# Two orders of small work around the second block of a fused retention and ELU layer kernel: where the last weight sums are made, and which ScalarE work goes first at the change of layers

## The chip, the cores and the metric

The kernel runs on one core of one Trainium2 chip. The metric is the device time of one execution in microseconds; the time before is the median of six runs. In the profile the engines are PE (TensorE: matrix products; PEld its weight loads), DVE (VectorE), ACT (ScalarE), POOL (GpSimd) and SP, which here only issues DMAs. "L532" is line 532 of the kernel before. Every engine carries out its own list of instructions strictly in the order in which the program emits them, and waits where an operand, or the buffer that it writes, is not ready.

## The reference

For each of 4 batches and 8 heads (768 positions, 64 dimensions) a state is decayed and fed, and read by the query; the heads are then put side by side to 3072 tokens of 512, and two dense layers with an ELU between them follow:

```python
for t in range(S):
    state = gamma[None, :, None, None] * state + np.einsum('bhd,bhe->bhde', k[:, :, t], v[:, :, t])
    y[:, :, t] = scale * np.einsum('bhd,bhde->bhe', q[:, :, t], state)
x = np.ascontiguousarray(attn_out.transpose(0, 2, 1, 3)).reshape(B * S, H * D)
h = x @ w_in                                                     # 512 -> 2048
g = np.where(h > 0.0, h, alpha * (np.exp(np.minimum(h, 0.0)) - 1.0))
return (g @ w_out).astype(np.float32)                            # 2048 -> 512
```

All of it is float32.

## The kernel before

The 3072 tokens are cut into six blocks of 512 tokens. For each block the retention makes `xb` (the block's input, transposed), the first layer with its ELU makes the inner values `gq`, and the second layer makes 512 outputs per token. All instructions are emitted in an order written out by hand with Python generators: a `next(...)` emits the work up to the next `yield`, so the place of a `next` decides where that work stands in every engine's list. There is no scheduler.

Block 0 uses plain products (`plain_first`, `plain_second`). While `plain_second` runs, the output weights arrive in eight pieces (`n` = 0 to 7), are decoded on DVE, and are combined there into the sums that later blocks need. From block 1 on, each product of two matrices is done in seven products of half the size instead of eight, after the Strassen-Winograd scheme. This needs sums of weight quarters (made once) and sums of input quarters.

The second layer goes one level deeper: each of its seven products is itself done in seven small products. The weights of these small products are sums of sums. `combine_w_out(at, low, high)` (L524 on) makes them for two neighbouring pieces: eight DVE `tensor_tensor` instructions (helper line L532), a `yield` after each, and at the end of each four the stores to a scratch tensor are put in the list `to_send` (issued by SP from L528). For the last pair of pieces (`at` = 3) four instructions of 128x512 come first (called s1 to s4 here, tile `wi`), and then four of 128x384 (m1 to m4). In the kernel before, L509 emits the first two of them, s1 and s2, at the end of the last step of `plain_second`, ahead of the copies of the last two output banks that fall to DVE (L519). The other six are left in `held["last"]`.

Block 1's first layer is four "quadruples" (`first(n)`, n = 0 to 3, each two row blocks of the inner layer), each by the general seven-product generator `strassen` (L587). It emits product 1, product 2, 6, 7, 5, then stops at `yield "gap"`, and later product 3, product 4, a plain `yield "last"`, and the last ELU of the quadruple, that of the quarter C21. The helpers:

- `kept(ps)` (L575): ACT copies a PSUM bank to a tile `m`, so that the bank or the sum can be used on.
- `plus(ps, m)` (L580): DVE adds a bank and a kept tile into `h`. It frees the bank.
- `elu(g, h)`: two ACT instructions (L444, L445), and an instruction on DVE that finishes the ELU (L448), which is put into `later` and emitted one ELU later, or by `flush()`.
- `combine_w_in(n)` (L559): four DVE sums of input weights for quadruple n.
- `combine_small(j)` (L700): eight POOL instructions in all on the input weights, after the last `combine_w_in`; L637 makes two sums on DVE of each quadruple's results.

The banks in use are a (two buffers), b and d. Products 1, 6, 5, 3 add up in one buffer of bank a; products 7 and 4 add up in bank d. So product 5 can start only when ACT has copied the sum of products 1 and 6, and product 7 of the next quadruple only when `plus` (L580) has read bank d after product 4 of this one.

The loop over quadruples runs the last part of quadruple n - 1 (`tail`: products 3 and 4 with their ELUs) after products 1 and 2 of quadruple n, and hands out two steps of `sides[n]` per product:

```python
sides = [
    itertools.chain(combine_w_in(1), last), itertools.chain(combine_w_in(2), combine_w_in(3)), iter(()), iter(()),
]
```

So in quadruple 0 DVE's list has the four sums of `combine_w_in(1)` and then what is left of `last`, with the `plus` and ELU instructions of the quadruple between them. `send_small()` issues the stores at the end of the quadruple.

After quadruple 3, the second layer starts with `second_twice(1, ...)`. Its first large product j = 1 has the small products 1 and 2, then 6 and 7, then 5, and so on (`inner`, matmuls at L834, ACT copies `ms` at L842, DVE sums at L846). The order at the change of layers in the kernel before is: small products 1 and 2, the tail of quadruple 3 with products 3 and 4 and its last ELU, `flush()`, then small products 6 and 7, and then 5.

Of the kernel before, what the change touches and what calls it, by code (L numbers as in the profile page):

```python
# [17 lines left out]
def kernel(  # L18
# [47 lines left out]
    NF = DFF // P // 2  # L66
# [350 lines left out]
    def combine_x_parts():  # L417
        sub = lambda o, x, y: nc.vector.tensor_tensor(out=o, in0=x, in1=y, op=ALU.subtract)
        b11, b12, b21, b22 = (xb[:, 2 * r : 2 * r + 2, half[t]] for r in range(2) for t in range(2))
        sub(xt[0], b12, b11)  # L420
        yield
        sub(xt[1], b22, xt[0])
        yield
        sub(xt[2], b22, b12)
        yield
        sub(xt[3], b21, xt[1])
# [8 lines left out]
    def flush():  # L435
        while later:
            later.pop(0)()
# [46 lines left out]
    def plain_second():  # L484

        ops = [bank(x).rearrange("p a b -> p (a b)") for x in "aabd"]
        for n, f in enumerate(ORDER_F):
            wo = decoded[2 * NQ + n]
            for row in range(2):
                for d in range(4):  # L490
                    nc.tensor.matmul(  # L491
                        ops[d], lhsT=wo[:, row, (d if row else d ^ 2) * P :][:, 0:P], rhs=g_plain[row * NF + f],
                        start=(n == 0 and row == 0), stop=(n == NF - 1 and row == 1),
                    )
            so = t4.tile([P, 4, 256], FP32, name="so", tag="t4")
            tt = lambda o, x, y, op: nc.vector.tensor_tensor(out=o, in0=x, in1=y, op=op)
            a21, a11, a12, a22 = (wo[:, r, 256 * d : 256 * d + 256] for r in range(2) for d in range(2))
            tt(so[:, 0], a21, a22, ALU.add)
            tt(so[:, 1], so[:, 0], a11, ALU.subtract)
            tt(so[:, 2], a11, a21, ALU.subtract)  # L500
            tt(so[:, 3], a12, so[:, 1], ALU.subtract)
            nc.sync.dma_start(quarters(f)[:, 8:16], so.rearrange("p a (d c) -> p (a d) c", c=P))
            if n < 5:
                send_small()
            sources = wo.rearrange("p r (d c) -> p (r d) c", d=2)[:, 1:4], so
            if n % 2:
                last = combine_w_out(n // 2, low, sources)

                for _ in itertools.islice(last, 8 if n < NF - 1 else 2):  # L509
                    pass  # L510
            low = sources
            if n >= 5:
                send_small()
            held["last"] = last if n % 2 else None
            yield
        for d in range(4):
            ot = gq["T3"][:, 2 * d : 2 * d + 2, :]
            eng = (nc.scalar.copy, nc.vector.tensor_copy)[d % 2]
            eng(ot.rearrange("p a b -> p (a b)"), ops[d])  # L519
            nc.sync.dma_start(out[0, d // 2, :, :, d % 2, :].rearrange("t p c -> p t c"), ot)  # L520
# [5 lines left out]
    def send_small():  # L526
        while to_send:
            nc.sync.dma_start(*to_send.pop(0))  # L528

    def combine_w_out(at, low, high):  # L530

        tt = lambda o, x, y, op: nc.vector.tensor_tensor(out=o, in0=x, in1=y, op=op)  # L532
        if at < 3:

            ms = [mpool.tile([P, 2, TH], FP32, name="m", tag="m") for _ in range(4)]
            ms = [m.rearrange("p a (b c) -> p (a b) c", c=P)[:, 0:3] for m in ms]
            ss = gq["T3"].rearrange("p (k f) (b c) -> p k (f b) c", k=4, c=P)
        else:
            ms, ss = (stage.tile([P, 4, 4, P], FP32, name="wi", tag="stage") for _ in range(2))
            ms = [ms[:, k, 0:3] for k in range(4)]  # L540
        ss = [ss[:, k] for k in range(4)]
        for first, dst, k in [(0, ms, 0), (3, ss, 1)][:: 1 if at < 3 else -1]:
            a11, a21, a12, a22 = (x[k][:, :, P * d : P * d + P] for x in (low, high) for d in range(2))
            s1, s2, s3, s4 = dst
            tt(s1, a21, a22, ALU.add)
            yield
            tt(s2, s1, a11, ALU.subtract)
            yield
            tt(s3, a11, a21, ALU.subtract)
            yield  # L550
            tt(s4, a12, s2, ALU.subtract)
            to = scratch2[first : first + dst[0].shape[1]].rearrange("j p (k f c) -> k f p j c", k=4, f=4)
            for k in range(4):
                to_send.append((to[k, at], dst[k]))
            yield
# [14 lines left out]
    def bank(x):  # L570
        return ps_f.tile([P, 2, TH], FP32, name="p" + x, tag=x, bufs=2 if x == "a" else 1)
# [90 lines left out]
    for tb in range(1, NTB):  # L662
# [5 lines left out]
        for j in ORDER2:  # L668
            last = (4, 3) if j == 4 and tb == NTB - 1 else (3, 4)
# [377 lines left out]
    for n, _ in enumerate(plain_second()):  # L1047
        decode_all()
        prepare()
        if n == 1:  # L1050
            scores(1, 0)
            scores(1, 1)
        elif n == 2:
            states(1, 0)
            states(1, 1)
        elif 3 <= n <= 5:
            outputs_step(1, n - 3)
        elif n == 6:
            combine_x()
            for _ in combine_w_in(0):  # L1060
                pass
# [17 lines left out]
    tail = iter(())  # L1079
    last = held["last"]  # L1080
# [4 lines left out]
    for n in range(NQ):  # L1085
# [14 lines left out]
        tail = cur  # L1100
# [13 lines left out]
    sec = second_twice(1, combine_x_twice)  # L1114
    for _ in range(3):
        next(sec)
    for _ in tail:
        pass
    flush()
    next(sec)  # L1120
    for step, s in enumerate(sec):
        if step in (0, 2, 4, 5):
            retention_step(2, (1, 1, 2, 2, 3, 4)[step])
# [2 lines left out]
    tail = sec  # L1126


    for tb in range(2, NTB):
# [24 lines left out]
        tail, parts = iter(()), combine_x_parts()  # L1154
        for at, j in enumerate(TWICE):
# [14 lines left out]
            tail = cur  # L1170
# [3 lines left out]
        sec = second_twice(tb, combine_x_twice if more else lambda: None)  # L1174
# [47 lines left out]
        tail = sec  # L1222
# [51 lines left out]
```

## Time and profile before

| what | value |
|---|---|
| median of six runs (lowest, highest) | 645.17 us (643.9, 645.48) |
| the profiled execution's own time | 647.54 us |
| its span | 645.7 us |
| outside the span (the difference) | 1.84 us |
| PE busy | 635.1 us, 98% of the span |
| DVE busy | 498.1 us, 77% |
| ACT busy | 241.4 us, 37% |
| POOL busy | 40.0 us, 6% |

A row of a timeline gives the start in us from the span's start, the busy time, the engine, the line, the operation, the tiles (written from read), the sizes and the count; at its end, in brackets, the idle time of the engine ahead of it and what ended this idle time. Rows that follow one another with the same shape are merged, and the last number of a merged row is its count.

Block 1's first layer lies between 143.4 and 199 us of the span, and its second layer between 191.6 and about 250 us.

### The profile page before, as it was taken

What the parts mean: (1) busy time and instruction counts of PE and PEld (TensorE: products, weight loads), DVE (VectorE), ACT (ScalarE), POOL (GpSimd) and SP (SyncE); (2) the same over time, 40 slices, a digit from 0 to 9 for tenths busy, and PEclk for the clock granted to TensorE, in tenths of its full rate; (3) what the DMA queues carried; (4) which work ended last, traced back from release to release, by engine and by line L of the source; (5) the groups of instructions that cost most, each with busy time, mean ns of one, the idle gap of its engine ahead of it and who ended that gap; (6) DMA issues with size and microseconds to landing.
All of it is one profiled execution on the core that took longest, in us unless ns stands there. A gap on an engine that the chain in (4) does not pass through costs nothing.

```text
span 645.7 us, 15901 instructions
## 1 busy us (share of the span) xinstructions
PE 635.1 (98%) x6526; PEld 542.6 (84%) x6526; DVE 498.1 (77%) x893; ACT 241.4 (37%) x465; POOL 40.0 (6%) x42
## 2 busy tenths in 40 slices
PE   8999999999999999999999999999999999999998
PEld 4764445458889999989999989999988999988997
DVE  6889699898979676589767488867578959557976
ACT  5576621204452112546111465211465311356311
POOL 1002100000450000100000110000020000000000
PEclk9999999999999999999999999999999999999999
DMA  8749778989486789702789820688840688710794
GB/s 297 292 157 375 249 228 235 319 247 277 167 275 224 243 259 319 279 3 65 238 279 300 297 82 20 222 277 279 294 170 2 197 264 264 227 47 1 214 310 163
DMA packets 85209, 139.72 MB, mean 216 GB/s; under 512 B 6672, under 2 KB 38800, under 8 KB 82832
## 3 DMA queue, kind: packets, MB, share of 16 engines
q1 hardware_dynamic: 85136, 138.70, 66.2%
q8 instruction: 52, 0.85, 0.5%
q14 instruction: 21, 0.17, 0.1%
HBM read 114.56 MB, written 24.12 MB: 215 GB/s over the span
## 4 chain that ended last, share of the span: by engine, by line
PE 87%; DVE 4%; DMA 4%; POOL 2%; issue 1%; ACT 1%; SPq 1%; DVEq 0%; POOLq 0%; ACTq 0%
PE pa L834 19%; PE pa L795 10%; PE pd L834 9%; PE hp L477 6%; PE pb L834 5%; PE pa L749 4%; PE pa L491 4%; PE pb L795 4%; PE qa L795 3%; DMA kvn<-in_qkv_dram 3%; PE pd L749 2%; PE qd L795 2%; PE pd L795 2%; PE pd L491 2%; PE pb L491 2%; PE y L364 2%
## 5 line engine op out<-in xcount | busy, mean ns | idle before, releaser
L842 ACT COPY ms<-pa 128x128 f32<-128x128 f32 x104 | 27.7, 266 | 145.7 <-PE pa L834 145.7
L834 PE MATMUL pa<-ts,wq 128*128 128x128 f32 x560 | 74.1, 275 | 0.3 <-ACT ms L842 0.3
L834 PE MATMUL pd<-ts,wq 128*128 128x128 f32 x552 | 73.2, 276 | 0.2 <-DVE res L846 0.2
L834 PEld LDWEIGHTS pa<-ts,wq 128*128 128x128 f32 x560 | 68.5, 192 | 0.8 <-ACT ms L842 0.5
L834 PEld LDWEIGHTS pd<-ts,wq 128*128 128x128 f32 x552 | 67.1, 192 | 0.7 <-DVE res L846 0.5
L834 PE MATMUL pa<-gC,wq 128*128 128x128 f32 x480 | 64.7, 278 | 0.0
L445 ACT ACTIVATE r<-r 128x512 f32<-128x512 f32 x96 | 60.5, 630 | 3.1
L834 PEld LDWEIGHTS pa<-gC,wq 128*128 128x128 f32 x480 | 59.0, 192 | 1.3
L444 ACT ACTIVATE r<-gC 128x512 f32<-128x512 f32 x64 | 39.9, 624 | 32.4 <-DVE gC L803 32.4
L846 DVE TENSOR_TENSOR res<-pd,ms 128x128 f32<-128x128 f32 x68 | 19.5, 287 | 37.6 <-PE pd L834 36.5
L269 POOL TENSOR_TENSOR kvn<-kvn,vf 128x512 f32<-128x512 f32 x21 | 25.3, 1210 | 328.4 <-DMA kvn<-in_qkv_dram 310.5
L448 DVE SCALAR_TENSOR_TENSOR gC<-r,gC 128x512 f32<-128x512 f32 x64 | 44.4, 726 | 0.7 <-ACT r L445 0.7
L711 DVE TENSOR_TENSOR ts<-gC,ts 128x512 f32<-128x512 f32 x60 | 41.3, 688 | 1.0
L711 DVE TENSOR_TENSOR ts<-gC 128x512 f32<-128x512 f32 x60 | 41.0, 684 | 0.0
L834 PE MATMUL pb<-gC,wq 128*128 128x128 f32 x240 | 33.0, 277 | 0.7 <-issue 0.6
L834 PEld LDWEIGHTS pb<-gC,wq 128*128 128x128 f32 x240 | 29.6, 192 | 1.6 <-DVE gC L448 0.8
L491 PE MATMUL pa<-gC,w_s 128*128 128x512 f32 x64 | 30.6, 600 | 0.0
L867 ACT COPY res<-pa 128x128 f32<-128x128 f32 x34 | 9.1, 266 | 57.6 <-PE pa L834 54.5
L803 DVE TENSOR_TENSOR gC<-qa,gC 128x512 f32<-128x512 f32 x8 | 5.5, 692 | 25.1 <-PE qa L795 18.3
L575 ACT COPY m<-pa 128x512 f32<-128x512 f32 x24 | 13.9, 580 | 25.3 <-PE pa L795 14.0
L795 PE MATMUL pa<-xt,w_s 128*128 128x256 f32 x96 | 23.0, 382 | 0.0
L795 PE MATMUL pa<-xt,w_b 128*128 128x256 f32 x96 | 23.0, 382 | 0.0
(226 smaller groups left out, 1238.1 us busy)
## 6 DMA issues: line engine op xcount, KB each, us to landing
wq<-scratch_dram SPq DMA_DIRECT2D x277, 256.0 KB, 4.4
wraw<-in_w_dram SPq DMA_DIRECT2D x16, 1024.0 KB, 6.5
qk<-in_qkv_dram SPq DMA_DIRECT2D x24, 512.0 KB, 6.4
kvn<-in_qkv_dram SPq DMA_DIRECT2D x24, 512.0 KB, 7.1
scratch_dram<-w_s SPq DMA_DIRECT2D x8, 512.0 KB, 4.9
scratch_dram<-so SPq DMA_DIRECT2D x8, 512.0 KB, 5.0
out_dram<-res SPq DMA_DIRECT2D x14, 256.0 KB, 4.3
scratch_dram<-gT SPq DMA_DIRECT2D x12, 256.0 KB, 4.3
```

The source lines that it names most:

```text
L269: eng.tensor_tensor(out=kv[:, 1], in0=kv[:, 1], in1=vf[:, i].unsqueeze(2).to_broadcast([C, H, D]), op=ALU.mult)
L444: nc.scalar.activation(e, h, AF.Relu, scale=-1.0)
L445: nc.scalar.activation(e, e, AF.Exp, scale=-1.0)
L448: nc.vector.scalar_tensor_tensor(g, e, -1.0, h, ALU.add, ALU.max)
L477: nc.tensor.matmul(hp, lhsT=w[n][:, fi, j // 2, j % 2, :], rhs=xb[:, j, :], start=(j == 0), stop=(j == 3))
L491: nc.tensor.matmul(ops[d], lhsT=wo[:, row, (d if row else d ^ 2) * P :][:, 0:P], rhs=g_plain[row * NF + f], start=(n == 0 and row == 0), s ...
L711: sub = lambda o, x, y: nc.vector.tensor_tensor(out=o, in0=x, in1=y, op=ALU.subtract)
L749: nc.tensor.matmul(ps[:, f, :], lhsT=lhs[f], rhs=xs[j][k], start=(begin and f == 0), stop=True, skip_group_check=True,)
L795: nc.tensor.matmul(ps[:, fi, :], lhsT=w[:, fi, j2, :], rhs=x[:, j2, :], start=(j in (1, 7) and fi == 0 and j2 == 0), stop=(j2 == 1), skip_ ...
L834: nc.tensor.matmul(ps, lhsT=w[:, f, :], rhs=ts[j][k][:, f, :], start=(begin and f == 0), stop=(f == 3), skip_group_check=True,)
L842: nc.scalar.copy(m, ps)
L846: nc.vector.tensor_tensor(out=o, in0=x, in1=y, op=ALU.add)
```

## The change

It has two parts. In `plain_second` the last step emits none of the eight sums of `combine_w_out(3)` instead of two; all eight are then emitted in quadruple 0 of block 1, two per product as before, after `combine_w_in(1)`. At the change of layers the tail of quadruple 3 is gone through step by step, and when it stops at `"last"`, ahead of the ELU of C21, the small products 6 and 7 are emitted with their copy. The `next(sec)` after `flush()` goes.

```diff
                 last = combine_w_out(n // 2, low, sources)
 
-                for _ in itertools.islice(last, 8 if n < NF - 1 else 2):
+                for _ in itertools.islice(last, 8 if n < NF - 1 else 0):
                     pass
...
     sec = second_twice(1, combine_x_twice)
     for _ in range(3):
         next(sec)
-    for _ in tail:
-        pass
+
+    for at in tail:
+        if at == "last":
+            next(sec)
     flush()
-    next(sec)
     for step, s in enumerate(sec):
```

## The prediction

> **What bounds the kernel now.** I read the page's busy line first.
>
> ```profile
> PE 635.1 (98%) x6526; PEld 542.6 (84%) x6526; DVE 498.1 (77%) x893; ACT 241.4 (37%) x465; POOL 40.0 (6%) x42
> ```
>
> PE is busy for all but 10.6 us of 645.7, so no edit of DVE or ACT work counts unless it moves a moment at which PE stands still. The change touches the stretch from 143 to 220 us, so next I read the waits of PE there (line waited for: total us, times, longest).
>
> ```profile
> PE y L390 <- issue: 1.2, 1, 1.2
> PE pa L625 <- ACT m L575: 0.4, 1, 0.4
> PE pa L834 <- ACT ms L842: 0.3, 1, 0.3
> PE pd L834 <- DVE res L846: 0.2, 1, 0.2
> ```
>
> The second and third waits are the two at which the two parts aim. Start to start they cost more than the idle figure, since a matmul's end is modelled: products of the first layer follow each other every 1.73 us, those of the second layer every 0.89 us, and the first step after a wait is another 0.10 us late, because its weight load is then not hidden. The timeline shows how the wait at 150.92 comes about, and what DVE does afterwards.
>
> ```profile
> 145.85 0.69 DVE L532 TENSOR_TENSOR wi<-so 128x512 f32<-128x512 f32 x1
> 146.58 0.69 DVE L532 TENSOR_TENSOR wi<-wi,so 128x512 f32<-128x512 f32 x1
> 147.19 0.68 DVE L519 COPY gT<-pa 128x512 f32<-128x512 f32 x1
> ...
> 148.38 0.68 DVE L580 TENSOR_TENSOR h<-pb,m 128x512 f32<-128x512 f32 x1
> ...
> 149.10 0.63 ACT L444 ACTIVATE r<-h 128x512 f32<-128x512 f32 x1 [3.19 <-DVE h L580]
> 149.76 0.63 ACT L445 ACTIVATE r<-r 128x512 f32<-128x512 f32 x1
> 150.30 0.57 ACT L575 COPY m<-pa 128x512 f32<-128x512 f32 x1
> ...
> 150.92 1.99 PE L625 MATMUL pa<-xt,w_b 128*128 128x256 f32 x8 [0.40 <-ACT m L575]
> ...
> 153.57 0.69 DVE L580 TENSOR_TENSOR h<-pd,m 128x512 f32<-128x512 f32 x1 [1.12 <-ACT m L575]
> ```
>
> The two sums s1, s2 stand in front of two copies, the `plus`, an ELU and the copy that product 5 needs. But DVE then has a long list in this layer, and two quadruples later PE waits for DVE:
>
> ```profile
> 169.91 3.12 DVE L448 SCALAR_TENSOR_TENSOR gC<-r,h 128x512 f32<-128x512 f32 x2
> 172.95 0.68 DVE L580 TENSOR_TENSOR h<-pd,m 128x512 f32<-128x512 f32 x1
> 173.55 0.67 DVE L448 SCALAR_TENSOR_TENSOR gC<-r,pa 128x512 f32<-128x512 f32 x1
> 174.25 1.69 DVE L637 TENSOR_TENSOR gT<-gC,gC 128x512 f32<-128x512 f32 x1
> ```
>
> Product 7 of quadruple 2 starts at 173.68, 0.05 after the end of that L580. It was due at 171.74 + 1.73 = 173.47, so it lost 0.21. This is where the end of DVE's list sets PE.
>
> **First part, the gain.** DVE's row before the sums starts at 145.40; rows of DVE that need nothing of the one just before follow each other in 0.60 us (0.34 at this half size), others in 0.72. Without s1 and s2 the copies L519 start at 145.74 and 146.34. The `plus` needs product 2, started at 145.13; the row pair 179.04 (PE) and 181.03 (DVE) puts 2.00 between them, so it starts at 147.12, not 148.38. ACT follows 0.72 later (as 148.38 to 149.10): L444 at 147.84, L445 at 148.50, the copy from 149.04 to 149.61. Product 5 is due at 148.58 + 1.73 = 150.31 and no longer waits; it gains 0.61, and the next product 0.10 more: 152.03 for 152.75, a lead of 0.71.
>
> **First part, the debt.** The `plus` of C22 at 153.57 waits for ACT's copy after product 5, so it moves 0.71 up, to 152.85. Of the eight sums DVE's list now has only s1 ahead of it (before: s3), though DVE stands idle there for longer than the 1.12 shown. Behind it stand one L448, s2, s3, s4 and m1 to m4; before it was one L448, s4 and m1 to m4. Two more at 0.60 make 1.20, less the 0.71: the next `plus` comes at 157.86 for 157.37, 0.49 late. From there to 177.6 DVE pauses once, 0.76 ahead of the L448 at 159.42, and this waits for an ELU that starts from that same late `plus`. So the 0.49 is carried. Two products meet it:
> - Product 7 of quadruple 1 is due 0.71 early, at 160.67, but writes bank d, which the L580 at 160.02 + 0.49 = 160.51 must have read: 161.19 plus 0.05 is 161.25 (before 161.38). With the late first step the next product comes at 161.25 + 1.83 = 163.08 for 163.11. The lead is used up to 0.03.
> - Product 7 of quadruple 2 already waits for DVE, so it takes the 0.49 in full: 174.17 for 173.68. From there to 189.5 PE has no pause in which to win it back.
>
> First part: +0.49 us. If DVE won its 0.49 back between 161.3 and 173, -0.13 would remain; if nothing of the 0.71 helped, +1.20, two sums at 0.60. I take +0.49, since every row on the way is in the trace.
>
> DVE is late at 172.95 because of POOL: its sums L700 run from 169.52, and beside them L448 with two inputs in SBUF takes 1.44 and 1.67 and L637 1.69 (0.69 without POOL), while L448 and L580 with one input in PSUM keep 0.67 and 0.68. The moved sums have two SBUF inputs, but run near 154 to 156, 14 us ahead of POOL, so they keep 0.60. And POOL's first sum starts 0.13 after DVE's last L559 ends (169.39), so it moves with DVE.
>
> The Trainium skill (SBUF — State Buffer, Who interferes with whom) has this as a lock: a VectorE instruction with two SBUF inputs and a GpSimd instruction that reads SBUF exclude each other, and the second to start waits. The rows agree. The rule speaks against whatever delays DVE's list here: by it, one more of DVE's instructions caught behind POOL would add the length of a POOL instruction, 1.28 to 1.72 by the rows of L700, and an estimate of this part by that page is +1.8 to +2.2.
>
> The queues: SP's list keeps its order. The stores of s1 to m4 (L528) wait for their data: s1 at 151.2 as before, s2 at 154.8 instead of 151.65, the last at 158.2 instead of 158.04. Behind it SP issues the next input loads at 158.61, now near 158.8; POOL reads them after 181.6, so that is free. The out stores of the two copies come 1.4 earlier, ahead of any reader.
>
> **Second part.** These rows carry it:
>
> ```profile
> 197.87 0.63 ACT L444 ACTIVATE r<-h 128x512 f32<-128x512 f32 x1 [1.24 <-DVE h L580]
> 198.53 0.63 ACT L445 ACTIVATE r<-r 128x512 f32<-128x512 f32 x1
> 199.06 0.25 ACT L842 COPY ms<-pa 128x128 f32<-128x128 f32 x1
> ...
> 199.36 0.97 PEld L834 LDWEIGHTS pa<-ts,wq 128*128 128x128 f32 x8 [0.51 <-ACT ms L842]
> ```
>
> The listing of both programs' orders shows that of this part only ACT's list changes: one copy of small product 6 goes ahead of L444 and L445. PE's, DVE's, POOL's and SP's lists have it as before, the two weight fetches included. Small product 6 starts at 196.90 and its copy can run 1.09 later (as 206.14 to 207.23), at 197.99. Product 7 starts at 197.89, so 5 is due at 197.89 + 0.99 = 198.88 instead of 199.37, and the states behind it (L326), due 0.99 later, at 199.87 instead of 200.45: 0.59. Behind the copy now wait the ELU's two ACT steps, 0.38 later: they end at 199.54, and DVE, which needs them for L448, has its own work until 199.80. So this is covered by 0.2; without the cover it would cost at most the 0.38.
>
> What is late next is DVE. Its sum L846 at 200.86, which had waited 0.38 for ACT, can start when that L448 (199.80) lets it, at 200.40: 0.46 earlier. From there DVE's list runs without a pause to the L846 at 207.01 that frees bank d; product 7 at 207.35 had waited for it and comes 0.46 earlier, not 0.59. Behind it PE waits for no other engine. Second part: -0.46, bounds -0.59 (PE's full gain) and +0.38 (ELU uncovered).
>
> **Sum.** +0.49 - 0.46 = +0.03. On the profiled execution: span 645.70 + 0.03 = 645.73, with the 1.84 outside 647.57 (before 647.54). That execution lies 2.37 above the median of the six runs; on the median the sum is 645.2. With the bounds the sum could be -0.13 - 0.59 = -0.72 to 1.20 + 0.38 = +1.58; both terms at their ends at once is not likely, so the forecast's own range is 644.8 to 646.0. About 0.2%, 1.3 us, is what a measurement of this kernel can tell from no change.
>
> **Rivals.**
> 1. The debt is paid within the first layer: -0.13 - 0.46 = -0.59, 644.6. For it: DVE is busy only 12.1 of the 12.3 us from 161.4 to 173.7. Against it: the little idle time there is behind waits of its own list. Still no difference that can be told.
> 2. Slower, one mechanism: a further pause of PE for its own program. The first wait shown above, "issue" in L390, is 1.40 us from 216.97 to 218.38 with no engine to blame. The trace's packets have one of the 52 of the instruction queue started at 214.95 that took 2.23 us, where most take 0.9 to 1.0. It falls in a burst of 64x64 products, 128 in 2.0 us. So the point is a packet that takes over about 2 us ahead of such a burst. The second part moves the burst L326 at 200.45 by 0.6 against the weight fetches on SP. A second pause there costs 1.40: 646.6. Against it: the packet at 202.86 took 0.97.
> 3. The same pause is gone, since the traffic beside it is shifted: 643.8. For both: the six runs lie in two groups, 643.9 and 644.09, and 645.14 to 645.48, 1.2 apart, about one such pause.
>
> The Trainium skill (Runtime: NRT & Kernel Launch, Instruction fetch mechanics) says that the fetch of the program is hidden, because dispatch is slower than the refill. By it rivals 2 and 3 would be worth nothing; the pause in the trace speaks against it for bursts of tiny products.
>
> That the change does not do what it says is excluded: the order listing has the sums and the copy in their new places.
>
> **How the numbers follow.** Forecast 0.52; rival 1 0.10; rival 2 0.19; rival 3 0.16; 0.03 for anything larger. Forecast and rival 1 lie within 0.2% (643.9 to 646.5), so 0.61 with a little off for the forecast's upper bound; slower 0.21 (rival 2, and that bound); faster 0.18 (rival 3, and part of the rest). The range reaches to rivals 2 and 3: 643.6 to 646.7.
>
> **What would show it.** In the profile after: product 5 near 150.3 with no wait for ACT; the `plus` of quadruple 1 near 157.9; waits of PE for DVE L580 near 161.2 and, longer than before, near 174.2; the copy L842 ahead of L444 near 198.5, no wait of small product 5 for ACT; product 7 of j = 2 still waiting for L846, at the time it had before. The first part is wrong if product 7 of quadruple 2 starts before 173.7; the second if the PE step from small product 7 to 5 is not 0.99. A gain over 1 us with these rows as told would mean rival 3, and I would look for the 216.97 pause.

## The result: 0.3% slower, outside the range, with the rows where the sum put them

| | before | after |
|---|---|---|
| median (lowest, highest; executions) | 645.41 us (643.52, 650.49; 76) | 647.54 us (644.5, 651.7; 36) |
| ratio after to before, 95% interval | | 1.0031 [1.002, 1.0042] |
| the profiled execution's time, its span | 647.54, 645.7 us | 648.44, 646.7 us |

The forecast was 645.2 with a range up to 646.7. The median lies 0.84 above that range. Of all the executions told of below, four took 813 to 1104 us at a far lower mean clock; they are left out of every ratio, and the two of them that were profiled (the kernel before again, and the same with 64 added products) are not read.

In the profile after, the waits of PE between 143 and 225 us are these (line waited for: total us, times, longest):

```profile
PE y L390 <- issue: 2.1, 1, 2.1
PE pd L625 <- DVE h L580: 0.9, 2, 0.5
PE pd L834 <- DVE res L846: 0.3, 1, 0.3
```

Both waits for ACT are gone, as the change intends. Two waits for L580 stand in the place of the first, and the pause of PE that no engine explains is longer, 2.1 for 1.2 us. The timeline of after shows the first part's rows:

```profile
146.43 0.68 DVE L519 COPY gT<-pa 128x512 f32<-128x512 f32 x1
147.03 0.68 DVE L519 COPY gT<-pd 128x512 f32<-128x512 f32 x1
148.02 0.69 DVE L580 TENSOR_TENSOR h<-pb,m 128x512 f32<-128x512 f32 x1 [0.31 <-PE pb L625]
...
151.20 1.89 PE L625 MATMUL pa<-xt,w_b 128*128 128x256 f32 x8
...
153.75 0.69 DVE L580 TENSOR_TENSOR h<-pd,m 128x512 f32<-128x512 f32 x1 [1.66 <-ACT m L575]
...
158.76 0.68 DVE L580 TENSOR_TENSOR h<-pb,m 128x512 f32<-128x512 f32 x1
...
162.15 1.99 PE L625 MATMUL pd<-xt,w_s 128*128 128x256 f32 x8 [0.43 <-DVE h L580]
...
175.07 1.13 PE L625 MATMUL pd<-xt,w_s 128*128 128x256 f32 x4 [0.49 <-DVE h L580]
```

All these times lie 0.90 later than in the profile of before, from a place ahead of everything that the change moves: the first 31 us, in which PE waits for inputs, took 0.90 us longer in this execution. I call this shift of PE at 31 us the head of an execution, and take it off. Then product 5 starts at 150.30 (150.31 was worked out), the `plus` of quadruple 1 at 157.86 (157.86), product 7 of quadruple 1 at 161.25 (161.25) and that of quadruple 2 at 174.17 (174.17). The second part's rows:

```profile
199.38 0.27 ACT L842 COPY ms<-pa 128x128 f32<-128x128 f32 x1 [1.36 <-PE pa L834]
199.54 0.63 ACT L444 ACTIVATE r<-h 128x512 f32<-128x512 f32 x1
...
200.27 1.06 PE L834 MATMUL pa<-ts,wq 128*128 128x128 f32 x8
...
208.27 1.16 PE L834 MATMUL pd<-ts,wq 128*128 128x128 f32 x8 [0.27 <-DVE res L846]
```

The copy runs ahead of the ELU, small product 5 has no wait, and product 7 at 208.27 (207.37 without the head) has the time of before plus 0.02. So up to here the structure costs +0.02, where +0.03 was forecast. Then comes the pause, in before (first row) and in after:

```profile
218.38 0.34 PE L390 MATMUL y<-qk,kvn 64*64 64x64 f32 x6 [1.20 <-issue]
...
217.67 0.44 PE L390 MATMUL y<-qk,kvn 64*64 64x64 f32 x12
220.22 0.34 PE L390 MATMUL y<-qk,kvn 64*64 64x64 f32 x6 [2.11 <-issue]
```

From start to start it took 2.33 us, in the profile of before 1.41. A second pause of before, near 315 us (0.84 with the late step behind it), is not there. The spans add up: head +0.90, structure +0.02, first pause +0.91, second pause -0.84, together +0.99; the spans differ by 1.0. So in the profiled pair no more than 0.02 is work that was moved, the two pauses together add 0.07, and the rest is the head. Of the 2.13 between the medians this pair explains little.

### The profile page after: what moved, and what is told of

Same layout as the page of the kernel before. It is cut to its first block, busy times and chain, and to the rows that moved or that the text cites. A ratio compares the mean times of both kernels' runs of the same rounds, so it can differ in the third digit from the quotient of the medians.

```text
span 646.7 us, 15903 instructions
## 1 busy us (share of the span) xinstructions
PE 634.0 (98%) x6526; PEld 542.1 (84%) x6526; DVE 497.5 (77%) x893; ACT 241.0 (37%) x465; POOL 40.5 (6%) x42
## 4 chain that ended last, share of the span: by engine, by line
PE 87%; DVE 4%; DMA 4%; issue 2%; POOL 2%; SPq 0%; ACT 0%; DVEq 0%; POOLq 0%; ACTq 0%
PE pa L834 19%; PE pa L795 10%; PE pd L834 9%; PE hp L477 6%; PE pb L834 5%; PE pa L749 4%; PE pa L491 4%; PE pb L795 4%; PE qa L795 3%; PE pd L749 2%; PE qd L795 2%; PE pd L795 2%; PE pd L491 2%; PE pb L491 2%; PE y L390 2%
## 5 line engine op out<-in xcount | busy, mean ns | idle before, releaser
L846 DVE TENSOR_TENSOR res<-pd,ms 128x128 f32<-128x128 f32 x68 | 19.5, 287 | 37.2 <-PE pd L834 36.5
L448 DVE SCALAR_TENSOR_TENSOR gC<-r,gC 128x512 f32<-128x512 f32 x64 | 43.5, 711 | 0.7 <-ACT r L445 0.7
```

Source lines behind the costliest of these rows:

```text
L448: nc.vector.scalar_tensor_tensor(g, e, -1.0, h, ALU.add, ALU.max)
L846: nc.vector.tensor_tensor(out=o, in0=x, in1=y, op=ALU.add)
```

## The experiments

Each kernel ran twelve times beside the kernel before on the same chip, unless the text says otherwise; an interval is a 95% interval of the ratio. "Both" is the changed kernel.

### The kernel before again, each part alone, and both

For the sums alone only the count of `islice` changes, for the ELU only the order at the change of layers:

```diff
-                for _ in itertools.islice(last, 8 if n < NF - 1 else 2):
+                for _ in itertools.islice(last, 8 if n < NF - 1 else 0):
```
```diff
-    for _ in tail:
-        pass
+    for at in tail:
+        if at == "last":
+            next(sec)
     flush()
-    next(sec)
```

> The kernel before, unchanged, timed against itself: how far two identical programs lie apart, and whether the pauses of PE with no engine to blame (1.40 us at 216.97, 0.75 at 314.39, 0.53 at 530.76 in the first profile) come back at the same places. Theory A (the pause at 217 is set by how the weight fetches lie against the burst of small products): the same pause within 0.3 us, ratio 1.000 within 0.001. Rival B (these pauses are chance): another pause length or place, while the ratio is still 1.000.

> The first part alone: all eight sums in quadruple 0. By the rows of the prediction PE is 0.49 us later from 174 on: ratio 1.0008. Theory A (the first part costs its 0.49 and the rest comes from the second part): 645.9 at a median of 645.4 for before, and the pause at 217 as long as before (1.4). Rival C (the first part carries the whole loss of 2 us): 647.5.

> The second part alone: the copy of small product 6 ahead of the last ELU. The rows say -0.46 us at 207. Theory A (PE comes earlier against the weight fetches and pays a longer pause for its program near 217, 2.3 us instead of 1.4, or more in the runs without a profile): slower, 646.4 to 647.5, with that pause in its profile. Rival C (the first part carries the loss): 645.0.

> The changed kernel again, with a second profile. Theory A: slower by about 2 us (1.003) and a pause of about 2.3 us near 218 again. Rival B (pauses are chance): the same ratio, but the pause of another length or elsewhere, so that the loss must lie in something that the profile does not show.

The kernel before had a median of 646.08 here (35 executions). The four came out at 646.01 (ratio 1.0003 [0.9981, 1.0025]), 646.54 (1.0005 [0.9987, 1.0023]), 646.65 (1.0004 [0.9987, 1.0021]) and 647.87 (1.0011 [0.9988, 1.0033]). By the ratios none can be told from the kernel before, and an interval of 0.2% to each side is wider than every term of the sum. In the traces of the last three the rows separate the parts cleanly. Of the sums alone, the waits of PE:

```profile
PE y L390 <- issue: 1.0, 1, 1.0
PE pd L625 <- DVE h L580: 0.9, 2, 0.5
PE pa L834 <- ACT ms L842: 0.3, 1, 0.3
```

and of the ELU alone:

```profile
PE y L390 <- issue: 1.5, 1, 1.5
PE pa L625 <- ACT m L575: 0.3, 1, 0.3
PE pd L834 <- DVE res L846: 0.3, 1, 0.3
```

Each part takes its wait for ACT away and puts the wait for DVE there that the prediction named. With the head taken off, PE stands 0.72 ahead after product 5 and 0.49 behind after 173.68 with the sums alone; with the ELU alone it gains 0.48 at 199.37, of which 0.44 is left at 208.

### The cuts between the packets of PE's program

The trace shows PE's program coming in 52 packets of 16 KB on the instruction queue, for 13311 instructions of PE that it records (weight loads, products and semaphore instructions): 256 for each packet. In every trace with the pause near 217 us, but for those of the 64 products below, PE stands at the same instruction, its 4033rd. The pause near 315 us stands at the 6337th, and one that the ring of 8 below has near 532 us at the 11457th: 9 and 29 packets further. So I take these places to be the first instructions of packets. I laid PE's starts beside the packets. PE passes the cut before at 211.36 in the trace of before; the packet starts 3.60 us after that and ends 5.82 after it, but PE needs it after 5.62. PE goes on 1.2 us behind its end.

The first attempt to move the cut put unread 64x64 products at the start:

```diff
+    for _ in range(64):
+        nc.tensor.matmul(
+            warm[0:64, 0:64], lhsT=blank[0:64, 0:64], rhs=blank[0:64, 0:64], start=True, stop=True, skip_group_check=True
+        )
```

> The kernel before, with 64 products of 64x64 whose result nobody reads added to PE's list near 2.3 us, where PE waits for its first input. They shift where PE's program is cut into the 16 KB packets of the instruction queue by half a packet, so that the cut lies in the middle of the burst at 215.6 instead of ahead of it. Theory A: the pause near 217 (1.0 to 2.1 us in all five profiles so far) is gone, and the kernel is 1.0 to 1.4 us faster than before: 0.998. Rival B (the pause has another cause than the packet's cut): the pause stays, ratio 1.000.

> The first part alone with the same 64 products. Theory A: +0.5 us against the kernel before with these products, the debt of DVE alone. Rival B: the same +0.5, so this run is the scale for the other two.

> The second part alone with the same 64 products. Theory A (the part's 0.46 was lost, and more, in a longer pause at 217): with no pause it is 0.46 us faster than the kernel before with these products. Rival C (the copy ahead of the ELU costs by itself, in some way that a single profile does not show): +0.5 us as without the products.

> Both parts with the same 64 products. Theory A: within 0.3 us of the kernel before with these products (0.49 - 0.46), that is 0.998 of the kernel before. Rival C: slower than it by 1 to 2 us, as the changed kernel is against the kernel before.

It missed its aim. The 64 products added exactly 256 instructions to PE's program, one whole packet, so every cut stayed at the same work (the pause now stands at the 4289th instruction). The medians of these four, of six executions each, are 7 to 10 us longer; in the three traces that can be read PE's head is 4.89 to 12.45 us later. The ratios are 1.0081 [1.0056, 1.0107] for the kernel before with them, and 1.0122 [1.008, 1.0165], 1.0095 [1.0062, 1.0129] and 1.0142 [1.0102, 1.0182] for the sums, the ELU and both. Where the pause could be read, it stayed: 2.78 with the sums, 1.19 with the ELU, 2.55 with both. From their times I draw nothing, since what the products cost at the start is many times the terms in question.

The second attempt adds 76 instructions, less than a packet:

```diff
-    unread(2, TB)
+    unread(1, TH)
+    for _ in range(20):
+        nc.tensor.matmul(
+            warm[0:64, 0:64], lhsT=blank[0:64, 0:64], rhs=blank[0:64, 0:64], start=True, stop=True, skip_group_check=True
+        )
```

> The kernel before, its first warming product replaced by twenty products of 64x64 that nobody reads: PE's list gets 76 instructions longer (the 64 products of the runs before made 256, a whole packet, and so moved no cut at all against the work). PE's program comes in packets of 256 instructions; in every profile so far PE stops at its 4033rd instruction, between two packets, until about 1.4 us after the end of that packet. With 76 more this cut lies 38 small products earlier, in front of which PE has about 3 us more of work. Theory D (the pause near 217 is a late packet): no pause over 1 us near 217, a new short one possible at another cut; time within 1.5 us of before. Rival B (something else stops PE there): the pause of 1.2 to 2.8 us stays at the same product.

> Both parts with the same cut. Theory D (the rows of the two parts give +0.02, and the rest of the loss, 1 to 2 us, comes from the pause near 217, by its length and by the half-clock window of 3.41 us that can follow it): within 0.5 us of the kernel before with the same cut, and no larger share of executions with a clock of 0.997. Rival C (the loss lies elsewhere): 1.5 to 2 us slower than it.

The medians are 646.0 (ratio 0.9978 [0.9953, 1.0002]) and 646.17 (0.9986 [0.9962, 1.001]); the kernel before had 646.78 there. The pause near 217 is gone in both. (There is none near 315 either, but of the unchanged programs only the first profile of before had that one.) The waits of PE between 143 and 225 us are, with both:

```profile
PE pd L625 <- DVE h L580: 0.9, 2, 0.5
PE pd L834 <- DVE res L846: 0.3, 1, 0.3
```

and in the kernel before:

```profile
PE pa L834 <- ACT ms L842: 0.3, 1, 0.3
```

Two things follow. The pause hangs on where the cut falls: over all the traces read here 12 of 15 with unmoved cuts have it and none of three with moved ones. Three of the 15 miss it without a moved cut, so a single trace proves little. And the last list holds a surprise: the wait of product 5 for ACT, which the first part is there to remove, is gone from the kernel before too, although its two sums stand where they stood.

### The same two kernels once more

> The kernel before, one more profile, for the length of the pause near 217 (1.41 us in the first). Theory D: 1.0 to 1.6 us and the packet starting 3.5 to 4.5 us after its request.

> The changed kernel, one more profile and twelve more times. Theory D: a pause of 1.5 to 2.6 us near 218, a median 1 to 2 us above before, and the clock of 0.997 in two of five executions against one of four of before.

> The kernel before once more, for its pause near 217 us alone: 1.40 and 0 us in the two profiles so far. If its packet is as a rule earlier than that of the changed kernel (pauses of 2.33, 1.47 and 2.27), the pause is under 1.45 again; if the lateness is chance in both, it may be anything up to 2.8.

The kernel before, profiled twice, had no pause at all once (packet started 2.83 after the cut, ended 3.79 after it) and 1.96 the other time (5.19 and 6.15). Both had 2.27 and a median of 646.78, as had the kernel before beside it (ratio 0.9997 [0.9969, 1.0025]). In the second of these traces, the view by windows (its bounds, its length, busy time and count of PE, PEld, DVE, ACT and POOL, then granted clock, DMA share and GB/s) shows what can come behind a long pause:

```profile
216.00:220.00 4.00, 2.26 (x87) 2.05 (x78) 1.00 (x4) 0.00 (x0) 0.00 (x0) 1.00 0.70 246
220.00:224.00 4.00, 4.00 (x24) 4.00 (x23) 0.29 (x1) 0.53 (x2) 0.00 (x0) 0.57 0.43 114
224.00:228.00 4.00, 4.00 (x38) 4.00 (x37) 3.22 (x6) 0.53 (x2) 0.00 (x0) 1.00 0.72 230
```

PE ran at a granted clock of 0.5 for 3.41 us from 220.3 on, and its rows fell 1.63 us behind. It did not follow every long pause: the pauses of 2.27, 2.33 and, with the 64 products and the sums, 2.78 have no such stretch behind them. Nor is it a mark of the change: of the executions whose clock is on record, 22 of 59 of both and 52 of 138 of the kernel before had a mean clock of 0.997 or less. Of the kernels with moved cuts it was none of 36, the third of them told of below. But it blurs the medians: in this comparison the kernel before had 16 such executions of 29, both 2 of 12. Without them the medians are 646.08 and 646.66, not equal.

### The debt taken out, the cut moved, and fewer fetches in flight

```diff
-            next(sides[n], None)
-            next(sides[n], None)
+            for _ in range(3 if n == 0 else 2):
+                next(sides[n], None)
```

> The changed kernel, but quadruple 0 hands out three steps of the sides per product in place of two, so that s1 to s3 stand ahead of the plus of C22, where DVE is idle. By the rows there is then no debt: product 5 gains 0.6 to 0.7 as in the changed kernel, the next plus is not late, product 7 of quadruple 1 has no wait for L580, and with the second part's 0.46 the rows stand some 1.1 to 1.2 us ahead of the kernel before at 208 us. Theory 1 (the order is worth what its rows say, the pause of PE for its program near 217 us decides the rest): the pause stays, between 0 and 2.8 us, so the median is between 1.2 us faster and equal. Theory 2 (the order itself makes the changed kernel slower): the median stays 1 us or more above the kernel before, and the rows at 208 us do not lead.

> The same, with one warming product replaced by 20 tiny ones, so that the cuts between the packets of PE's program fall at other instructions. Theory 1: no pause near 217 us, and the rows of the three sums: 1.0 to 1.8 us faster than the kernel before in the median, the fastest of all the kernels here. Theory 2: as the kernel before or slower.

> The changed kernel with a ring of 8 tiles for the large input weights of the second layer in place of 11, so that fewer weight fetches are in flight at once. If the packet of PE's program near 217 us is late because it stands behind queued weight fetches, it starts under 3 us after PE passes the cut before it (2.8 to 5.9 so far) and the pause is under 0.8 us; the time falls to that of the kernel before or below, unless PE then waits for weights. If the number of fetches in flight does not matter, the start stays 2.8 to 5.9 us late and the pause 0.8 to 2.8.

With three steps per product s1, s2 and s3 stand in DVE's idle time before the `plus` of C22, and the debt is gone:

```profile
150.24 0.68 DVE L532 TENSOR_TENSOR wi<-so 128x512 f32<-128x512 f32 x1
150.96 0.69 DVE L532 TENSOR_TENSOR wi<-wi,so 128x512 f32<-128x512 f32 x1
151.57 0.68 DVE L532 TENSOR_TENSOR wi<-so 128x512 f32<-128x512 f32 x1
152.58 0.69 DVE L580 TENSOR_TENSOR h<-pd,m 128x512 f32<-128x512 f32 x1 [0.33 <-ACT m L575]
```

DVE still waits 0.33 for ACT there (1.66 in after), so the two sums that came forward cost nothing. No wait for L580 is left, and at 208 us PE stands 1.21 ahead, head taken off. All the same the median is 646.38 beside 646.83, ratio 1.0008 [0.9989, 1.0028]: a gain of over 1 us in the rows of one trace did not show in the time. Its trace has a pause of 1.45 near 217, and 7 of its 12 executions a clock of 0.997 or less.

With the cut moved as well, to another place (20 tiny products in place of `unread(2, TB)`) it has the lowest ratio of all: 644.95, ratio 0.997 [0.9952, 0.9987], the only one whose interval lies below 1. It beats the kernel before; the changed kernel as it is was not run beside it. The pause near 217 is gone, but a cut now falls at another place where its packet is late:

```profile
233.09 0.94 PE L834 MATMUL pa<-gC,wq 128*128 128x128 f32 x7 [1.44 <-issue]
```

The ring of 8 did not make the packet earlier: it started 4.78 us after the cut, and the pause was 1.72. The median is 648.66 (1.003 [1.0009, 1.005]), and its trace has PE's head 2.19 late. So in this one trace 8 weight fetches in flight in place of 11 did not make the packet earlier. The longer median is not explained: the trace also has a pause near 532 us (0.90 idle).

### Taking away the store that sets DVE's place

Why was product 5's wait gone in the kernel before with moved cut? I followed DVE's rows back. Up to 120 us DVE moves with PE. Near 124 us it waits for a store out of tile `m`, ahead of the third pair's sums, 1.97 us in before and 1.36 with the moved cut, and its place after that is the store's:

```profile
125.79 0.56 DVE L532 TENSOR_TENSOR m<-w_s 128x384 f32<-128x384 f32 x1 [1.97 <-DMA scratch_dram<-m]
```
```profile
126.49 0.56 DVE L532 TENSOR_TENSOR m<-w_s 128x384 f32<-128x384 f32 x1 [1.36 <-DMA scratch_dram<-m]
```

The first is of the kernel before, the second of the same with moved cut. There PE is 1.33 later and DVE, at 145.40, only 0.57: a lead of 0.76, more than the wait of 0.61. The last pair of kernels takes the store away:

```diff
-            ms = [mpool.tile([P, 2, TH], FP32, name="m", tag="m") for _ in range(4)]
+            pool, tag = (mpool, "m") if at < 2 else (hpool, "h")
+            ms = [pool.tile([P, 2, TH], FP32, name=tag, tag=tag) for _ in range(4)]
```

> The kernel before, but the third pair's four 128x384 sums go to tiles h (free then) in place of m, so that DVE no longer waits near 124 us for a store out of tile m (1.97, 1.82, 1.95, 1.85 and 1.36 us so far). Theory A (product 5's wait for ACT at 150.92, which the first part of the change removes, hangs on this store and not on the two sums alone): DVE is ahead by 0.6 us or more at 145, the wait is gone without any change of the sums' order, and the rows stand 0.6 to 0.7 us ahead from 152 us on, with no debt at 161 and 174. Theory B (the two sums ahead of the copies cost product 5 its 0.61 in any case): the wait stays within 0.2 us of 0.40.

> The changed kernel with the same other tiles. Theory A: its rows are those of the changed kernel (relative to the head: -0.72 at 152.75, +0.49 at 173.68, about 0 at 208), since its debt is made in quadruple 0; against the kernel before with the same tiles it is then 0.7 us behind at 208 us, and by as much slower but for the pauses near 217 us. Theory B: equal to the kernel before with the same tiles within 0.1 us at 208 us.

Theory A's condition did not come about. DVE starts the four sums 1.87 earlier, and then waits for the next store instead:

```profile
128.48 0.69 DVE L532 TENSOR_TENSOR gT<-so 128x512 f32<-128x512 f32 x1 [2.48 <-DMA scratch_dram<-gT]
```

Behind it DVE is 0.21 later than in before, PE 0.06, and product 5 waits as before, 0.41. So the wait in hand was the wrong one of two, and the pair does not settle what a kernel without either would do. One more trace speaks for the store all the same: in that of the ELU alone with the 64 products the wait for the store, which ends at 131.94 us there, is 2.61 us, and the copies L519 come so late behind it that PE waits 0.90 us for them ahead of product 7 of quadruple 0 and then 0.40 ahead of product 5. The medians are 645.18 (ratio 0.9981 [0.996, 1.0002]) and 646.67 (1.0002 [0.9981, 1.0022]), beside 646.08. Neither trace has a pause near 217, and their spans are 643.1 and 643.3.

### All traces side by side

PE's starts against the profile of before, head taken off, in us (worked out from the traces; the row names are times of before):

| kernel | head | 152.75 | 173.68 | 208.40 | pause near 217 |
|---|---|---|---|---|---|
| before | 0 | 0 | 0 | 0 | 1.41 |
| before, two further traces | -0.39, -0.01 | -0.16, -0.05 | -0.17, -0.06 | -0.06, -0.06 | 0, 1.96 |
| before, cut moved | +1.33 | -0.72 | -0.72 | -0.73 | 0 |
| before, other tiles | +0.06 | +0.16 | +0.17 | +0.19 | 0 |
| sums alone | -0.01 | -0.72 | +0.49 | +0.48 | 1.20 |
| ELU alone | +0.26 | -0.14 | -0.14 | -0.58 | 1.74 |
| ELU alone, 64 products | +4.89 | +1.22 | +1.21 | +0.72 | 1.19 |
| both | +0.90 | -0.72 | +0.49 | +0.02 | 2.33 |
| both, two further traces | +0.43, +0.34 | -0.72, -0.72 | +0.48, +0.49 | +0.03, +0.13 | 1.47, 2.27 |
| both, cut moved | +1.57 | -0.72 | +0.49 | +0.01 | 0 |
| both, other tiles | +0.49 | -0.72 | +0.50 | +0.03 | 0 |
| both, three steps | -0.27 | -0.71 | -0.72 | -1.21 | 1.45 |
| both, three steps, cut moved | +1.05 | -0.72 | -0.72 | -1.18 | 0 (1.71 at 233) |

The rows of both stand still from trace to trace. Those of the kernels with the first part left out do not: at 152.75 they lie anywhere between -0.72 and +1.22. The heads show something too: both have the later one in each like pair (0.90 to 0; 0.43 and 0.34 to -0.39 and -0.01; 1.57 to 1.33; 0.49 to 0.06), though with three steps it is -0.27. No instruction that the change moves stands there, and so few traces can fall like this by chance; but that the change leaves the head alone is argued, not shown.

## Why the prediction was wrong

- **First part, the gain: the size was right for one execution, and the term is not a constant.** Product 5 came at 150.30 as worked out. But the 0.61 was read from one trace. The wait behind it is a race between PE, which carries the head, and DVE, which is set anew by stores near 124 and 128 us. Against the further traces of the kernel before the gain is 0.56 to 0.67 with the late step for 0.72, against the one with moved cut it is 0, against the one with other tiles 0.88, and against the ELU alone with the 64 products 1.94.
- **First part, the debt: right,** to 0.01 at each of its two products. Where the gain is missing, the first part costs 0.49 + 0.72 = 1.21 instead of 0.49. That is the upper bound of 1.20 that the prediction kept, on another road: it had the lead wasted in the changed kernel, whereas here the kernel before has the lead already.
- **Second part: right.** Forecast -0.46 with L846 late next; measured -0.47 in after (from +0.49 to +0.02), -0.44 with the ELU alone, -0.49 with three steps, -0.36 in the last trace of both.
- **The sum of the structure** was +0.03 and is +0.02 in the profiled pair. Over the traces of the kernel before (two further ones, cut moved, other tiles) it is between -0.17 and +0.75. In the pair with moved cuts, where no pause covers it, the spans are 643.4 and 644.4: 0.74 from these rows and 0.24 from the head (their medians lie 0.17 apart).
- **The step that failed** is the one from the rows to the time: the sum took the wait, the pauses and the head of one execution as fixed, and gave their change no term. In the profiled pair the head grew by 0.90 and the pause near 217 by 0.91, and the one near 315 (0.84) went; over the traces the wait's worth moved as told above.
- **The rivals on the pause.** Rival 2 put 1.40 on a further pause at a burst that the second part moves; there was no further one, but the old one grew. Rival 3 had it gone, which a further trace of the unchanged kernel shows as well. The prediction treated as three cases what is one quantity with a wide scatter: 0 to 1.96 in the kernel before, 1.47 to 2.33 with both, 0 in each with other tiles. Three traces of each are too few to say that the change lengthens it. And the two groups that rival 3 saw in six times are not there in 76, which fill the range from 643.5 to 647.6 with no gap above 0.3 and reach 650.49.
- **The rule on instruction fetch** (the Trainium skill, Runtime: NRT & Kernel Launch, Instruction fetch mechanics, by which it is hidden) does not hold here: PE stood up to 2.78 us for a packet. The same section gives the size of 256 instructions per block, and the cut's place in the traces agrees.
- **The locks of DVE and POOL** (the same skill, SBUF — State Buffer, Who interferes with whom) did not catch one more instruction: behind the late L580 the two L448 take 3.12 as before, and L637 1.68 for 1.69. So the estimate of +1.8 to +2.2 by that page did not come about.

**What stays open** is the size of the loss in the median, and its cause. In the first comparison both were 2.13 slower than the kernel before, then 1.79, 0.00, 0.17 with moved cuts and 1.49 with other tiles. Part of the scatter is the clock: in the first comparison the 15 executions of both with a mean clock of 0.997 or less have a median of 649.08, the other 21 one of 647.08. Without such executions both are 0.81, 0.58, 0.17 and 1.43 slower in the four later pairs, always the same sign; the clocks of the kernel before in the first comparison are not on record. So a loss of some tenths to 1.5 us is likely even without such executions, but this does not show its cause. The pause cannot be all of it, for the last pair's traces have none. The missing gain of the first part (up to 0.72 against the kernel before) would be of the right size and sign; but the profiled executions of the kernel before mostly do have the wait that the first part removes, and what the unprofiled ones have can't be seen. I cannot divide the 2.13 among the pause, the missing gain, the clock and the head.

## What to carry to other kernels

A wait read from one trace is worth its length only if both sides of the race are set by the same thing; here one side came from the inputs' arrival and the other from a store, and further traces showed 0.28, 0.40 and, with a few more instructions at the head, no idle time at all. Where a step hands work to a later place, look for idle time that takes all of it: one more step per product ahead of a `plus` that waited 1.66 us anyway removed the whole debt. And where PE stops for no engine in a burst of tiny products, count its instructions: if two such places lie a multiple of 256 apart, as the 4033rd, 6337th and 11457th do here, suspect the cuts of the program. Here an edit elsewhere that added 76 instructions moved the cut out of the burst, 72 put one where PE stopped again (1.44 us near 233), and 256 moved nothing.

## What was not expected of the hardware

- PE's packets start at very different times against PE's own progress. In before, those for the cuts at 280 to 286 us start 0.5 to 2.2 us before PE passes the cut ahead of theirs; those for 191 to 245 us, beside weight fetches, start 1.3 to 4.6 us after it. Traffic alone does not order them: those for the cuts at 120, 160 and 189 us start 2.3 to 3.2 us before, in slices of the page that moved 275 to 319 GB/s. The cause of the lateness isn't settled: 8 fetches in flight instead of 11 left it at 4.78.
- The pause ends later than the packet: in after the packet ended 6.45 us after the cut and PE went on 7.94 after it.
- A store's wait that is taken away can come back as the next store's: 1.97 us at tile `m` became 2.48 us at tile `gT`.
